# A gated global filter on one core: the exchange read back by halves on alternate partitions, smaller last stores, and a new instruction order

## The chip, the cores and the metric

One core of one Trainium2 chip. The metric is device microseconds of one execution. A run whose time is over 1.5% above the fastest of the same kernel is called slow. The profile covers one execution; its span (first to last instruction) is shorter than that execution's time (before 115.6 against 117.37).

## The reference, cut to what matters

```python
def layer(x, w_r, w_i):                       # _A_ref and _B_ref, alike
    X = rfft2(x.astype(float32))              # x: [1, 2048, 1024] bf16
    return irfft2(X * (w_r + 1j * w_i), s=(2048, 1024)).astype(bfloat16)

def reference(A_x, A_w_r, A_w_i, B_x, B_w_r, B_w_i, gate_w):   # B_x is not used
    g = sigmoid((A_x * gate_w).sum(-1, keepdims=True))
    return g * layer(A_x, A_w_r, A_w_i) + (1 - g) * layer(A_x, B_w_r, B_w_i)
```

## The kernel before

The transforms are matrix products. One string, `ORDER`, lists every operation of the program, some 600 tokens, and each engine runs its share of it in that order. Semaphore waits are put in by the tile framework when the program is built, from what each operation reads and writes. The stages, by token:

- **Folds** `F1, FC, FD, FX, FP`: first transform of x, mirrored columns folded into the tile `y` by VectorE (DVE) and GpSimd (POOL).
- **Unit loop**, 16 units (units 0 to 7 are the even columns, 8 to 15 the odd ones): `F2, T, F3, X` (transform and copies), `P` (product with the weights on DVE), `J` (inverse product on TensorE, PE), `R` (copy of its result to a tile `rl` by ScalarE, ACT, or DVE), `H` (store of `rl` to scratch in DRAM).
- **Exchange**: rows and columns change places between `H` and the read back `L`. Even data goes to the tile `Re`, odd data to `Ro`, in eight blocks of 2,048 columns each.
- **After the loop**: `V` (inverse along rows with the gate masked in, on PE), `VC` (its copy), `C` or `U` (inverse along columns, on PE), `EX, EQ` (even results: a copy, then sum and difference on POOL), `OR, OP, QD, QP` (output rows from even results and odd products), `S` (store of a block).

The parts that the change and the argument touch:

```python
def exchange_row(t, i):
    return 8 * t + 4 * (i % 2) + i // 2
...
    Re = big.tile([P, NS1 * 1024], BF16, name="re")
    Ro = big.tile([P, NS1 * 1024], BF16, name="ro")
    RR = [r[:].rearrange("p (v r s f) -> p v r s f", v=8, r=2, s=2) for r in (Re, Ro)]
    EV = Re[:].bitcast(F32).rearrange("p (v s f) -> p v s f", s=2, v=8)   # even results lie over Re
    SC = [dm.tile([2 * NT, P, 512], BF16, name=f"sc{p}") for p in range(2)]
...
    def scratch_store(n, tt, q="S"):                                      # H
        n, tt = int(n), int(tt)
        a = 4 * (n % NU) + 2 * tt
        Q[q].dma_start(SC[n // NU][a:a + 2].rearrange("a p m -> p a m"), RLs[n][:, tt])

    def scratch_load(par, v, q="S"):                                      # L: 512 KB, all 128 partitions
        par, v = int(par), int(v)
        Q[q].dma_start((Re, Ro)[par][:, v * 2048:v * 2048 + 2048],
                       SC[par][:].rearrange("a (h v q) m -> (a h) v (q m)", h=4, v=8)[:, v])
...
    def even_mix(v, s, h, e):                                             # EQ, on POOL
        t = TM["X", v, s]
        Q[e].tensor_tensor(EV[:, v, s, 256 * h:256 * h + 256], t[:, 0], t[:, 1], (ALU.add, ALU.subtract)[h])
```

When the even data of block v has been used, its even result (f32) is written over the same columns of `Re`. Nearly all DMAs are issued by the sync engine's queue (SP), in the order of the list. A DMA that must wait holds up those behind it: in the changed kernel one read-back waited 3.6 us for POOL and was issued at 81.97 us, and the six stores behind it went out from 82.52 on (80.01 in e1, where that wait is gone).

Of the kernel before, what the change touches and what calls it, by code (L numbers as in the profile page):

```python
# [186 lines left out]
def gated_mix(ctx, tc, x_in, we_in, wo_in, w0_in, gw_in, out):  # L187
# [363 lines left out]
    def scratch_load(par, v, q="S"):  # L551

        par, v = int(par), int(v)
        Q[q].dma_start((Re, Ro)[par][:, v * 2048:v * 2048 + 2048],
                       SC[par][:].rearrange("a (h v q) m -> (a h) v (q m)", h=4, v=8)[:, v])
# [157 lines left out]
```

## Time and profile before

| | before |
|---|---|
| time, median of 3 runs | 117.17 us (117.02 to 118.86) |
| span of the profiled run, granted PE clock | 115.6 us, 0.985 |
| unit loop: last inverse group ends | 77.0 us |
| PE waits for the read-back | 0.8 us, once |
| last DVE row ends; span ends | 112.05; 115.6 us |

The prediction shows the lines. How to read them: in the stretches, one row is a piece of the span with the busy time of each engine, so an engine whose number equals the length of the piece is full. In the waits, a row is "engine, tile, line, what it waited for: us in total, times, longest". In a timeline, the bracket at the end is the idle time of the engine before the group and what ended it.

### The profile page before, as it was taken

The numbers are of one execution on the slowest core, as the hardware profiler recorded it, in microseconds if no ns is written. First come the engines' busy times: TensorE is split into PE (matmuls) and PEld (weight loads), VectorE is DVE, ScalarE is ACT, GpSimd is POOL, SyncE is SP. The second block draws the span as 40 slices with busy tenths as digits, with TensorE's granted clock in tenths as the row PEclk, the third lists the DMA queues.
The fourth block names the chain that finished last, engine by engine and source line by source line (L and its number), as shares of the span: only waits on it lengthen the run. The fifth ranks groups of instructions, "written<-read, shape, count | busy, mean of one in ns | idle before, by whom it ended". The sixth has DMA issues, their size and how long they took to land.

```text
span 115.6 us, 3953 instructions
## 1 busy us (share of the span) xinstructions
...
## 2 busy tenths in 40 slices
...
GB/s 90 348 326 401 403 374 367 363 397 408 210 222 324 371 394 373 169 263 397 350 293 354 348 306 401 254 357 382 352 353 411 403 418 98 198 346 119 327 279 181
DMA packets 17794, 36.79 MB, mean 318 GB/s; under 512 B 1904, under 2 KB 10736, under 8 KB 17776
## 3 DMA queue, kind: packets, MB, share of 16 engines
...
q10 hardware_dynamic: 288, 0.10, 0.4%
...
## 4 chain that ended last, share of the span: by engine, by line
PE 39%; DVE 19%; DMA 16%; ACT 16%; issue 4%; SPq 1%; DVEq 1%; ACTq 0%
ACT rl L204 11%; PE ps L581 9%; PE ps L565 8%; DVE y L382 7%; PE ps L450 6%; PE ps L334 5%; DMA sc<-rl 5%; DMA re<-sc 4%; DMA ig<-cst_ig 4%; PE ps L537 3%; DMA re<-in_x_dram 3%; PE ps L480 3%; DVE p L494 3%; ACT X L204 3%; PE ps L590 3%
## 5 line engine op out<-in xcount | busy, mean ns | idle before, releaser
L615 POOL TENSOR_TENSOR re<-wx 128x256 f32<-128x256 f32 x28 | 19.6, 730 | 55.3 <-DMA re<-sc 53.1
L204 ACT CAST rl<-ps 128x1024 bf16<-128x1024 f32 x29 | 29.6, 1142 | 0.7 <-ACT wx L204 0.7
L204 ACT COPY wx<-ps 128x256 f32<-128x256 f32 (+1 forms) x39 | 17.2, 498 | 10.5 <-PE ps L334 8.2
L537 PE MATMUL ps<-p,wj 32*64 32x512 bf16 x512 | 20.5, 381 | 2.5 <-ACT rl L204 2.0
L204 ACT CAST V<-ps 128x512 bf16<-128x512 f32 x25 | 13.8, 601 | 11.3 <-PE ps L565 8.4
L494 DVE TENSOR_TENSOR p<-X,ro 128x2048 bf16<-128x2048 bf16 x16 | 19.1, 1215 | 0.0
L450 PE MATMUL ps<-fd,y 128*128 128x256 bf16 x128 | 16.5, 273 | 0.4 <-ACT rl L204 0.4
L382 DVE TENSOR_TENSOR y<-ps,wx 128x256 bf16<-128x256 f32 x48 | 16.4, 412 | 0.1
L334 PEld LDWEIGHTS <-re 128*128 128x128 bf16 x256 | 15.2, 100 | 1.6 <-DMA re<-in_x_dram 1.0
L334 PE MATMUL ps<-f,re 128*128 128x128 bf16 x256 | 15.8, 224 | 0.3
L204 ACT CAST T<-ps 128x512 bf16<-128x512 f32 x26 | 15.5, 693 | 0.0
L537 PEld LDWEIGHTS <-wj 32*64 32x64 bf16 x512 | 8.4, 103 | 10.6 <-issue 7.5
L382 POOL TENSOR_TENSOR y<-wx 128x256 bf16<-128x256 f32 x16 | 11.1, 734 | 8.2 <-DVE wx L206 5.9
L635 DVE TENSOR_TENSOR ot<-re,ps 128x512 bf16<-128x512 f32 x22 | 13.8, 681 | 0.4
L450 PEld LDWEIGHTS <-y 128*128 128x128 bf16 x128 | 11.5, 97 | 4.1 <-issue 2.6
L581 PE MATMUL ps<-ig,V 128*128 128x512 bf16 x56 | 13.4, 380 | 0.0
L204 ACT CAST X<-ps 128x1024 bf16<-128x1024 f32 x12 | 13.2, 1118 | 0.0
L206 DVE COPY wx<-ps 128x512 f32<-128x512 f32 (+1 forms) x10 | 5.8, 578 | 7.4 <-PE ps L334 4.8
L480 PE MATMUL ps<-T,wf 64*64 64x256 bf16 (+1 forms) x128 | 10.2, 332 | 1.1 <-DVE np L514 1.0
L590 PE MATMUL ps<-ig,V 128*128 128x256 bf16 x72 | 9.7, 273 | 0.0
L494 DVE TENSOR_TENSOR p<-X,wx 128x2048 bf16<-128x2048 bf16 x8 | 9.4, 1217 | 0.0
L494 DVE TENSOR_TENSOR p<-X,y 128x2048 bf16<-128x2048 bf16 x8 | 9.3, 1215 | 0.0
...
## 6 DMA issues: line engine op xcount, KB each, us to landing
sc<-rl SPq DMA_DIRECT2D x32, 256.0 KB, 4.7
ro<-in_we_dram SPq DMA_DIRECT2D x8, 512.0 KB, 8.3
re<-sc SPq DMA_DIRECT2D x8, 512.0 KB, 6.1
ro<-sc SPq DMA_DIRECT2D x8, 512.0 KB, 7.7
re<-in_x_dram SPq DMA_DIRECT2D x7, 512.0 KB, 8.0
out_dram<-ot SPq DMA_DIRECT2D x7, 512.0 KB, 2.6
wx<-in_wo_dram SPq DMA_DIRECT2D x4, 512.0 KB, 6.6
y<-in_wo_dram SPq DMA_DIRECT2D x4, 512.0 KB, 5.0
```

The source lines that it names most:

```text
L204: nc.scalar.copy(out=out, in_=in_)
L334: nc.tensor.matmul(o, lhsT=lh, rhs=rh, start=(h == 0), stop=(h == 1))
L382: Q[e].tensor_tensor(yo[:, v, k:k + n, s1, :], a.rearrange("p (k c) -> p k c", c=4), b.rearrange("p (k c) -> p k c", c=4), op)
L450: nc.tensor.matmul(ps[:, v * 256:v * 256 + 256], lhsT=y[:, v, par, b, 2 * t:2 * t + 2, :, :].rearrange("p j s c -> p (j s c)"), rhs=C["FD" ...
L480: nc.tensor.matmul(view(ps[ho, tt * 512:(tt + 1) * 512], dst), lhsT=lh, rhs=view(T[hp(jh), tt, :], src), start=(w == 0), stop=(w == 1))
L494: nc.vector.tensor_tensor(p[:, r], xb, w, ALU.mult)
L537: nc.tensor.matmul(o, lhsT=lh, rhs=src[r, ri, wi, tt], start=(q == 0), stop=(q == 3))
L565: nc.tensor.matmul(ps[:, ch * 128:ch * 128 + 128], lhsT=RR[par][:, v, ch // 2, s, c0 + 256 * ab:c0 + 256 * ab + 128], rhs=Ew[:, s1, :], st ...
L581: nc.tensor.matmul(ps, lhsT=Vs[par, v][:, s, ch, :], rhs=rh, start=(ch == 0), stop=(ch == 3))
L590: nc.tensor.matmul(ps[:, o:o + 256], lhsT=Vs[par, v][:, s, ch, :], rhs=g[:, o:o + 256], start=(ch % 2 == 0), stop=(ch % 2 == 1))
L615: Q[e].tensor_tensor(EV[:, v, s, 256 * h:256 * h + 256], t[:, 0], t[:, 1], (ALU.add, ALU.subtract)[h])
L635: nc.vector.tensor_tensor(otile(v)[:, s, h, :], EV[:, v, s], PS["O", 1, v, s], (ALU.add, ALU.subtract)[h])
```

## The change

The intent is to start the read-back earlier. A half of a block needs only the first four of the eight units (or the last four), so it can be issued before the other units are stored. The new row order puts the two halves on alternate partitions; that this moves data faster than two halves of neighbouring partitions was the author's assumption, and e3 tests it. The last block's store is cut in three so that less remains after the last row. The order was made anew around this.

```diff
 def exchange_row(t, i):
-    return 8 * t + 4 * (i % 2) + i // 2
+    r = 8 * t + 4 * (i % 2) + i // 2
+    return 2 * (r % 64) + r // 64
...
-    def scratch_load(par, v, q="S"):
-        par, v = int(par), int(v)
-        Q[q].dma_start((Re, Ro)[par][:, v * 2048:v * 2048 + 2048],
-                       SC[par][:].rearrange("a (h v q) m -> (a h) v (q m)", h=4, v=8)[:, v])
+    def scratch_load(par, v, g, q="S"):
+        par, v, g = int(par), int(v), int(g)
+        Q[q].dma_start((Re, Ro)[par][g:P:2, v * 2048:v * 2048 + 2048],
+                       SC[par][16 * g:16 * g + 16].rearrange("a (h v q) m -> (a h) v (q m)", h=4, v=8)[:, v])
...
-    def store(q, v, s="b"):
+    def store(q, v, s="b", h="b"):        # h: one half of the columns of a row pair
...
 ORDER: the tail of the list (almost every line differs; cut)
-... S:S:3 OR:6:1:0 S:S:6
+... OR:7:0:1 S:S:7:0 OR:7:1:1 S:S:7:1:1 OR:7:1:0 S:S:7:1:0
```

Three small parts: the constant E is loaded in two pieces (120 and 8 partitions), the gate vector's load moves from ACT's queue to SP's, and one pair of mask operations (`GW`) moves from DVE to POOL.

More of the change, by code (lines that the diff above doesn't have):

```diff
@@ L24 @@
 ORDER = """
-warm:8 c:A:F1 c:A:gws tab:A x:S:0:1 x:S:1:1 x:S:2:2 x:S:4:2 x:S:6:2 x:S:8:2 x:S:10:2 x:S:12:2 x:S:14:2 c:S:FD:0:1
-F1:1:o:0 F1:1:e:1 FX:1:o:D F1:0:o:2 FC:1:e:D F1:0:e:3 FP:1:o FD:1:e F1:3:o:0 F1:2:e:4 FC:0:e:D F1:3:e:1 gc:P FD:0:e
-F1:2:o:5 FC:3:e:A FC:2:e:D F1:4:e:3 FD:3:e FX:2:o:A F1:5:o:6 FX:0:o:A FD:2:e F1:5:e:5 FC:4:e:A FP:0:o FX:3:o:A FD:4:e
-F1:6:e:1 FC:5:e:A F1:4:o:2 FD:5:e FC:6:e:A F1:7:e:0 FP:2:o c:S:WF:0:4 FD:6:e F1:6:o:3 W:S:0 FC:7:e:A F1:9:e:7 FD:7:e
-FX:6:o:A F1:8:e:1 FP:3:o FC:9:e:D c:S:WJ:0:4 F1:11:e:3 FD:9:e F1:10:e:0 c:S:w0 FC:11:e:A F1:7:o:4 c:S:PM FC:8:e:A
@@ L30 @@
-FP:6:o FD:11:e FX:5:o:A c:S:EZ F1:13:e:5 FC:10:e:A FD:8:e W:S:1 F1:12:e:6 FP:5:o FD:10:e c:S:WF:4:16 FC:12:e:A
-F1:14:e:1 FC:13:e:A FD:12:e FX:4:o:A F1:15:e:3 W:S:2 F1:15:o:0 FD:13:e FP:4:o FC:15:e:A F1:11:o:2 FC:14:e:A FD:15:e
-FC:15:o:A F1:8:o:6 c:S:WJ:4:16 F1:14:o:5 FD:14:e FC:8:o:A F1:10:o:3 neg:A:0:4 FD:15:o FC:14:o:A F1:12:o:7 FX:7:o:A
-F2:0:0:1 FD:8:o c:S:E FC:10:o:A FP:7:o FC:12:o:A F2:1:0:0 W:S:3 FD:14:o T:0:0:A F2:0:1:4 FC:11:o:A F2:1:1:6 FD:10:o
-T:1:0:A W:S:4 pw:P F1:13:o:1 T:1:1:A FD:12:o F1:9:o:0 T:0:1:A F3:1:5 FD:11:o c:S:FD:1:2 FC:9:o:A F3:0:3 FC:13:o:A
@@ L35 @@
-FD:9:o X:1:A W:S:5 F2:3:1:2 FD:13:o F2:2:0:7 X:0:A F2:3:0:0 P:1:0 W:S:6 Y:1:1 F2:2:1:5 T:3:0:A Y:0:3 neg:A:4:16 GH:4
-P:1:1 W:S:7 T:2:0:A T:2:1:A NA:1:D N:1:D P:0:0 T:3:1:A GC:A NA:0:D P:0:1 F3:2:0 F2:4:0:5 X:2:A F2:4:1:2 F3:3:6 J:1:3:0
-T:4:0:D T:4:1:A X:3:A P:2:0 Y:2:2 GT:0:5 R:1:0:A F2:5:0:6 Y:3:7 NA:2:D P:2:1 T:5:0:A H:1:0 F3:4:2 c:S:IG R:1:1:A
-GT:1:5 W:S:8 F2:5:1:4 N:0:D NA:3:D P:3:0 X:4:A J:0:6:0 W:S:9 T:5:1:A H:1:1 N:2:D GT:2:5 P:3:1 R:0:0:A Y:4:2 GT:3:5
-F3:5:3 W:S:10 R:0:1:A N:3:D H:0:0 F2:7:1:6 GK:D NA:4:D P:4:0 F2:6:1:2 X:5:A GZ:0:0 F2:6:0:5 P:4:1 GS:0 W:S:11 F2:7:0:7
@@ L40 @@
-T:7:0:A T:7:1:D J:2:3:0 T:6:0:A GW:D:4 T:6:1:A Y:5:6 GW:D:0 R:2:0:A N:4:D NA:5:D P:5:0 R:2:1:A H:2:0 W:S:12 H:0:1
-P:5:1 F3:7:6 J:3:2:4 X:7:A H:2:1 F3:6:0 R:3:0:A F2:8:0:6 X:6:D F2:8:1:7 R:3:1:A F2:9:0:2 Y:7:3 T:8:0:D Y:6:0 T:8:1:A
-GZ:1:4 NA:6:D T:9:0:A P:7:0 J:4:6:0 GS:1 F2:9:1:2 N:5:D P:7:1 R:4:0:A T:9:1:A H:4:0 P:6:0 J:5:4:6 W:S:13 R:4:1:A H:3:0
-NA:7:D N:7:D R:5:0:A H:4:1 P:6:1 F3:8:2 F3:9:0 R:5:1:A F2:11:1:4 X:8:D F2:10:0:5 X:9:A H:5:1 F2:10:1:6 H:3:1 N:6:D
-F2:11:0:7 W:S:14 P:8:0 T:10:0:A J:6:2:0 T:11:0:A T:11:1:A T:10:1:D R:6:0:A P:8:1 J:7:4:6 R:6:1:A H:6:0 F3:10:2 H:5:0
@@ L45 @@
-P:9:0 R:7:0:A P:9:1 R:7:1:A H:7:0 J:8:0:4 X:10:A GW:D:12 H:7:1 F2:12:0:6 H:6:1 F2:12:1:7 W:S:15 R:8:0:A T:12:0:D
-P:10:0 R:8:1:A J:9:2:0 P:10:1 T:12:1:A H:8:1 F3:11:4 H:8:0 R:9:0:A F2:13:1:6 X:11:D R:9:1:A H:9:0 F3:12:2 F2:14:0:7
-X:12:A H:9:1 F2:13:0:0 L:0:0 F2:14:1:1 L:0:1 T:13:0:A T:13:1:D P:11:0 L:0:2 J:10:4:2 L:0:3 T:14:0:A P:11:1 T:14:1:A
-F3:13:6 R:10:0:A P:12:0 X:13:A H:10:0 J:11:0:4 L:0:4 P:12:1 R:10:1:A F3:14:6 R:11:0:A X:14:D F2:15:0:2 F2:15:1:3
-T:15:0:A P:13:0 T:15:1:A J:12:0:6 R:11:1:A V:0:0:1:2 P:13:1 R:12:0:A F3:15:4 V:0:0:0:3 R:12:1:D X:15:A H:12:0
@@ L50 @@
-V:0:1:0:0 H:10:1 V:0:1:1:1 L:0:5 VC:0:1:0:A P:14:0 H:11:0 J:13:4:6 VC:0:0:0:A VC:0:1:1:A P:14:1 VC:0:0:1:A R:13:0:A
-P:15:0 J:14:0:2 R:13:1:A H:13:0 H:11:1 C:0:0:1:4 P:15:1 H:12:1 C:0:0:0:5 EX:0:0:D R:14:0:D R:14:1:A EX:0:1:A H:14:1
-J:15:6:2 H:13:1 EQ:0:1:0:P V:0:2:0:4 EQ:0:0:0:P C:0:1:1:5 R:15:0:D R:15:1:A H:14:0 C:0:1:0:0 EQ:0:0:1:P H:15:1
-V:0:2:1:1 VC:0:2:0:A GW:D:8 V:0:3:1:2 H:15:0 EX:1:1:A L:0:6 V:0:3:0:3 VC:0:2:1:A EX:1:0:D L:0:7 EQ:1:1:0:P C:0:2:0:4
-VC:0:3:0:D VC:0:3:1:A C:0:2:1:1 EQ:1:0:0:P V:0:4:1:0 EX:2:1:D EQ:0:1:1:P V:0:4:0:5 C:0:3:0:2 EQ:2:1:0:P VC:0:4:0:A
@@ L55 @@
-C:0:3:1:1 EX:2:0:A V:0:5:0:3 EQ:1:1:1:P VC:0:4:1:A V:0:5:1:5 EQ:1:0:1:P VC:0:5:0:A C:0:4:0:4 VC:0:5:1:A EQ:2:0:0:P
-L:1:0 C:0:5:0:0 EX:4:0:D L:1:1 C:0:4:1:3 L:1:2 E:3:0:D EQ:4:0:0:P L:1:3 V:0:6:0:5 EX:4:1:A L:1:4 C:0:5:1:4 L:1:5
-EQ:2:0:1:P VC:0:6:0:D V:0:6:1:2 L:1:6 EX:5:0:D EQ:4:0:1:P V:0:7:1:3 VC:0:6:1:A V:0:7:0:5 EX:5:1:A EQ:5:0:0:P C:0:6:0:0
-L:1:7 C:0:6:1:2 EQ:2:1:1:P EX:6:1:A EQ:5:1:0:P VC:0:7:0:A VC:0:7:1:D E:3:1:D C:0:7:1:3 V:1:0:0:1 V:1:0:1:4 EQ:4:1:0:P
-VC:1:0:0:A C:0:7:0:2 VC:1:0:1:D EX:6:0:A EQ:6:1:0:P U:1:0:0:1 EX:7:0:A EQ:6:1:1:P V:1:1:0:0 OC:0:0:A EQ:5:0:1:P
@@ L60 @@
-V:1:1:1:2 VC:1:1:0:D U:1:0:1:4 EQ:6:0:0:P V:1:2:0:5 EQ:7:0:0:P V:1:2:1:0 VC:1:2:0:A EQ:7:0:1:P U:1:1:0:1 VC:1:2:1:D
-VC:1:1:1:A EQ:4:1:1:P EX:7:1:A U:1:2:0:5 OP:0:0:0 OR:0:1:1 OC:1:0:A OR:0:1:0 U:1:1:1:0 OR:2:0:0 EQ:6:0:1:P V:1:3:0:1
-U:1:2:1:4 OP:0:0:1 VC:1:3:0:A V:1:3:1:2 V:1:4:0:1 OP:1:0:0 OR:1:1:0 OR:2:0:1 OR:2:1:1 S:S:0 VC:1:3:1:A OR:1:1:1
-C:1:3:0:3 VC:1:4:0:A V:1:4:1:5 OR:2:1:0 EQ:7:1:0:P C:1:3:1:0 VC:1:4:1:A QD:3:0:0 S:S:2 U:1:4:0:1 OP:1:0:1 QD:3:1:1
-V:1:5:0:2 QD:3:1:0 OC:4:0:A V:1:5:1:4 EQ:5:1:1:P S:S:1 VC:1:5:0:A QD:3:0:1 U:1:4:1:5 OP:4:0:0 VC:1:5:1:D U:1:5:0:0
@@ L65 @@
-OR:4:1:0 OP:4:0:1 U:1:5:1:1 OR:5:0:0 OR:4:1:1 V:1:7:0:4 QP:3:0:0:P V:1:6:1:2 OR:5:0:1 S:S:4 VC:1:7:0:A V:1:7:1:3
-OR:5:1:1 U:1:7:0:4 VC:1:7:1:A EQ:7:1:1:P OR:5:1:0 V:1:6:0:0 QP:3:1:1:P OR:7:0:0 S:S:5 U:1:7:1:1 VC:1:6:0:A OR:7:0:1
-VC:1:6:1:A QP:3:1:0:P U:1:6:0:0 S:S:7:0 OR:7:1:1 OR:7:1:0 U:1:6:1:2 QP:3:0:1:P OR:6:0:0 S:S:7:1 OR:6:1:1 OR:6:0:1
-S:S:3 OR:6:1:0 S:S:6
+warm:8 c:A:F1 tab:A x:S:0:1 x:S:1:1 x:S:2:2 x:S:4:2 x:S:6:2 x:S:8:2 x:S:10:2 x:S:12:2 x:S:14:2
+c:S:FD:0:1 F1:0:e:0 F1:0:o:1 FC:0:e:A F1:1:e:2 FX:0:o:D FC:1:e:D F1:3:e:3 FD:0:e F1:3:o:1 FD:1:e F1:1:o:4
@@ new lines @@
+FX:3:o:A F1:2:e:0 FX:1:o:D FP:3:o F1:2:o:2 FC:2:e:A F1:5:e:1 FD:2:e F1:4:e:4 FC:5:e:A FP:0:o F1:4:o:5
+FC:3:e:A FD:5:e FC:4:e:A F1:7:e:0 FD:4:e F1:6:e:6 FP:1:o c:S:WF:0:4 FD:3:e FC:6:e:A F1:9:e:1 W:S:0
+FC:7:e:A F1:8:e:4 FD:6:e FC:9:e:A F1:6:o:3 FC:8:e:A FD:9:e c:S:WJ:0:4 F1:10:e:7 FX:4:o:A F1:7:o:6 FD:7:e
+c:S:w0 FP:4:o FC:10:e:A F1:11:e:1 c:S:PM FX:6:o:A FD:10:e F1:5:o:0 c:S:gws FX:2:o:A FD:8:e F1:13:e:3
+c:S:EZ FC:11:e:A FP:2:o F1:12:e:2 FD:11:e FC:13:e:A F1:15:e:7 FD:13:e F1:14:e:4 FP:6:o FC:15:e:A F1:14:o:1
@@ new lines @@
+FD:15:e FC:14:e:A F1:11:o:3 W:S:1 FX:5:o:A FD:14:e F1:9:o:5 c:S:WF:4:16 FC:12:e:A FP:5:o FC:14:o:A F1:13:o:0
+FC:11:o:A FD:12:e FX:7:o:A F1:10:o:4 W:S:2 FD:11:o FC:9:o:A F1:12:o:7 FP:7:o FC:13:o:A c:S:WJ:4:16 F2:1:0:2
+FC:10:o:A FD:14:o FC:12:o:A F1:8:o:3 c:S:E T:1:0:A FD:10:o F2:0:0:6 gc:P W:S:3 neg:A:0:4 F2:0:1:1
+FC:8:o:A FD:9:o T:0:0:A F2:1:1:2 W:S:4 FD:12:o T:0:1:A F1:15:o:4 pw:P T:1:1:A FD:8:o F3:0:5
+FC:15:o:A F3:1:1 FD:13:o c:S:FD:1:2 X:0:A F2:2:0:3 FD:15:o W:S:5 F2:2:1:7 X:1:A F2:3:0:0 P:0:0
@@ new lines @@
+Y:0:6 T:2:0:A GH:4 W:S:6 T:3:0:A NA:0:D P:0:1 neg:A:4:16 W:S:7 T:2:1:A F2:3:1:5 N:0:D
+P:1:0 GC:A F3:2:0 T:3:1:A J:0:2:6 c:S:IG X:2:A P:1:1 F3:3:4 R:0:0:A GT:0:0 P:2:0
+GT:3:0 Y:1:1 R:0:1:A Y:2:2 F2:5:0:3 P:2:1 X:3:A F2:4:0:6 F2:5:1:7 NA:1:D NA:2:D T:5:0:A
+N:2:D P:3:0 J:2:4:1 T:4:0:A T:5:1:A GT:1:0 N:1:D R:2:0:D R:2:1:A H:2:1 P:3:1 F3:5:6
+F2:7:0:3 X:5:A GT:2:0 J:1:1:4 W:S:8 GK:A H:0:0 F2:4:1:0 T:7:0:D R:1:0:A Y:3:6 Y:5:7
+T:4:1:D F2:7:1:3 R:1:1:A NA:3:D NA:5:D F3:4:0 N:3:D P:5:0 F2:6:0:2 T:7:1:A H:1:1 J:3:4:6
@@ new lines @@
+H:0:1 T:6:0:A P:5:1 W:S:9 X:4:A GZ:0:2 N:5:D R:3:0:A R:3:1:D F3:7:0 X:7:A H:3:0
+F2:6:1:4 P:4:0 H:1:0 Y:4:5 GZ:1:6 GS:0 W:S:10 NA:4:D H:2:0 P:7:0 T:6:1:A W:S:11
+J:5:0:2 GS:1 H:3:1 P:4:1 F3:6:4 R:5:0:A F2:9:1:6 W:S:12 N:4:D F2:9:0:7 GW:D:4 F2:8:0:0
+T:9:0:D T:9:1:A R:5:1:A W:S:13 Y:7:1 NA:7:D P:7:1 F3:9:6 X:6:A F2:8:1:1 N:7:D X:9:A
+GW:D:0 J:7:2:4 T:8:0:D T:8:1:A F2:11:1:6 P:6:0 R:7:0:A F2:11:0:7 H:7:0 P:6:1 J:4:0:2 H:5:0
+H:5:1 T:11:0:D T:11:1:A R:7:1:A Y:6:6 R:4:0:A NA:6:D N:6:D P:9:0 R:4:1:A P:9:1 F3:11:4
@@ new lines @@
+J:6:0:6 X:11:A H:4:1 F2:13:1:2 L:0:0:0 F2:13:0:3 R:6:0:A L:0:1:0 F3:8:4 P:11:0 H:4:0 X:8:A
+L:0:2:0 F2:10:0:0 P:11:1 H:7:1 F2:10:1:1 R:6:1:A T:13:0:D T:13:1:A H:6:1 J:11:4:6 T:10:0:A T:10:1:D
+H:6:0 P:8:0 L:0:3:0 J:9:2:0 R:11:0:A W:S:14 R:11:1:D R:9:0:A P:8:1 F3:10:4 X:10:A H:9:0
+F2:12:1:6 H:11:0 F2:12:0:7 R:9:1:A F3:13:2 P:10:0 T:12:0:A H:9:1 J:8:4:0 GW:D:12 T:12:1:A W:S:15
+X:13:A L:0:0:1 P:10:1 F2:15:0:7 H:11:1 F2:15:1:6 R:8:0:A L:0:1:1 F3:12:2 R:8:1:D L:0:4:0 T:15:0:A
+F2:14:0:4 T:15:1:A L:0:2:1 P:13:0 F2:14:1:5 X:12:A J:10:0:6 L:0:3:1 P:13:1 T:14:0:A L:0:4:1 F3:15:2
@@ new lines @@
+R:10:0:A P:12:0 T:14:1:A L:0:5:1 X:15:A V:0:0:0:4 L:0:5:0 P:12:1 F3:14:0 R:10:1:A V:0:0:1:5 VC:0:0:0:D
+VC:0:0:1:A H:10:1 J:13:2:6 P:15:0 X:14:A H:8:0 H:8:1 C:0:0:0:4 P:15:1 R:13:0:A L:0:6:1 C:0:0:1:5
+H:10:0 EX:0:0:A J:12:0:2 P:14:0 H:13:0 EX:0:1:A EQ:0:1:0:P V:0:2:0:4 R:13:1:D R:12:0:A V:0:1:0:5 EQ:0:0:0:P
+VC:0:1:0:A V:0:1:1:0 VC:0:2:0:D H:13:1 EQ:0:1:1:P R:12:1:A V:0:2:1:1 L:0:6:0 P:14:1 J:15:4:6 EQ:0:0:1:P VC:0:2:1:A
+H:12:1 VC:0:1:1:A H:12:0 R:15:0:A R:15:1:D J:14:2:0 GW:P:8 H:15:0 C:0:1:0:4 R:14:0:D R:14:1:A H:15:1
@@ new lines @@
+C:0:2:1:5 C:0:1:1:6 EX:1:0:A H:14:1 C:0:2:0:7 EX:1:1:D EX:2:1:A H:14:0 V:0:3:0:0 EQ:1:0:0:P EX:2:0:A L:0:7:0
+V:0:4:0:1 EQ:1:1:0:P VC:0:3:0:A L:0:7:1 V:0:3:1:6 V:0:4:1:7 L:1:0:0 EQ:2:0:0:P VC:0:3:1:A C:0:3:0:0 L:1:1:0 EQ:2:1:0:P
+C:0:3:1:6 E:3:0:A V:0:5:1:2 EQ:2:1:1:P VC:0:4:0:A VC:0:4:1:D V:0:5:0:0 EQ:1:1:1:P C:0:4:0:1 VC:0:5:0:A VC:0:5:1:D C:0:4:1:3
+EQ:1:0:1:P EX:4:0:D C:0:5:1:2 L:1:0:1 EX:4:1:A V:0:6:1:0 EQ:4:0:0:P L:1:1:1 EX:5:1:A C:0:5:0:1 L:1:2:0 EQ:4:1:0:P
+V:0:6:0:3 L:1:3:0 V:0:7:0:2 L:1:2:1 EQ:4:0:1:P VC:0:6:0:A VC:0:6:1:D E:3:1:D V:0:7:1:0 L:1:3:1 VC:0:7:0:A C:0:6:1:4
@@ new lines @@
+EQ:4:1:1:P L:1:4:1 VC:0:7:1:D C:0:6:0:3 L:1:4:0 EQ:5:1:0:P EX:5:0:D C:0:7:0:2 C:0:7:1:0 EQ:2:0:1:P EX:6:1:D EX:7:0:A
+V:1:0:0:1 L:1:5:0 EX:6:0:A EQ:5:0:0:P V:1:0:1:5 VC:1:0:0:D L:1:5:1 V:1:1:0:2 EQ:5:0:1:P VC:1:0:1:A V:1:1:1:3 VC:1:1:0:D
+U:1:0:0:1 EQ:5:1:1:P VC:1:1:1:A EQ:6:1:0:P U:1:0:1:2 OC:0:0:A EQ:6:0:0:P U:1:1:1:3 EQ:6:0:1:P U:1:1:0:1 EQ:6:1:1:P V:1:2:0:4
+OP:0:0:0 OR:0:1:0 OR:0:1:1 EX:7:1:D OC:1:0:A V:1:3:1:2 VC:1:2:0:A V:1:3:0:0 OP:0:0:1 V:1:2:1:1 VC:1:3:0:A U:1:2:0:4
+VC:1:3:1:A OP:1:0:0 OR:1:1:1 OR:1:1:0 VC:1:2:1:D S:S:0 C:1:3:0:0 OR:2:0:0 L:1:6:1 C:1:3:1:1 L:1:6:0 QD:3:0:0
@@ new lines @@
+U:1:2:1:5 OP:1:0:1 L:1:7:0 QD:3:1:0 V:1:4:0:2 QD:3:1:1 V:1:5:0:3 QP:3:0:0:P S:S:1 VC:1:4:0:A V:1:4:1:6 QD:3:0:1
+L:1:7:1 U:1:4:0:1 OR:2:0:1 VC:1:4:1:A QP:3:0:1:P VC:1:5:0:A OR:2:1:1 U:1:4:1:0 OR:2:1:0 V:1:5:1:4 QP:3:1:1:P S:S:2
+U:1:5:0:5 VC:1:5:1:A OC:4:0:A V:1:6:0:2 QP:3:1:0:P U:1:5:1:3 VC:1:6:0:A V:1:6:1:1 OP:4:0:0 OR:4:1:1 OR:4:1:0 OR:5:0:0
+OR:5:0:1 S:S:3 OR:5:1:0 U:1:6:0:0 VC:1:6:1:A OR:5:1:1 EQ:7:0:0:P V:1:7:0:2 S:S:5 OR:6:0:0 U:1:6:1:1 OP:4:0:1
+VC:1:7:0:A OR:6:0:1 V:1:7:1:3 OR:6:1:0 U:1:7:0:0 EQ:7:0:1:P S:S:4 VC:1:7:1:A OR:6:1:1 EQ:7:1:0:P U:1:7:1:2 S:S:6
@@ L69 @@
+OR:7:0:0 EQ:7:1:1:P OR:7:0:1 S:S:7:0 OR:7:1:1 S:S:7:1:1 OR:7:1:0 S:S:7:1:0
 """
@@ L259, in load_c @@
             Q[q].dma_start(C[n][:], gw_in)
+        elif n == "E":
+            for g in (slice(0, 120), slice(120, P)):
+                Q[q].dma_start(C[n][g], dr[n][g])
         elif n == "w0":
```

6 lines of the change are left out of this document (5 added, 1 removed).

## The prediction

> **What bounds the kernel now.** The cores view shows one core, 115.6 us, clock 0.985, so no throttle matters. I read the busy time by stretch first. The cuts are the first VectorE (DVE) work (5.94), the end of the folds (23), the start of the last group of inverse products (L537, near 77), the landing of the last even read-back (85) and the last stretch of TensorE (PE) work.
>
> ```profile
> 23.00:77.00 54.00, 49.94 (x988) 29.44 (x981) 53.02 (x73) 53.40 (x73) 0.86 (x3) 1.00 0.94 325
> 77.00:85.00 8.00, 7.79 (x103) 6.87 (x100) 5.38 (x9) 5.68 (x11) 6.89 (x11) 1.00 1.06 366
> 85.00:108.30 23.30, 22.68 (x237) 16.32 (x238) 17.72 (x29) 11.99 (x23) 22.24 (x27) 1.00 0.72 288
> 108.30:115.60 7.30, 1.73 (x8) 0.58 (x6) 3.67 (x6) 0.26 (x1) 2.09 (x2) 0.76 0.66 262
> ```
>
> The columns are PE, weight loads, DVE, ScalarE (ACT), GpSimd (POOL), then clock, DMA share, GB/s. There are three stages with three limits. From 23 to 77, the loop over the 16 units, DVE (53.0 of 54) and ACT (53.4) are both full; PE's 49.9 is waiting between short groups. From 77 on PE is full (30.5 of 31.3) while DVE and ACT have gaps, and POOL, idle in the loop, is full after 85. From 108 on nothing but the tail runs. So the end is: loop (ACT and DVE), then PE work left over, then tail. Next, the waits by cause and the queue's own waits:
>
> ```profile
> POOL re L615 <- DMA re<-sc: 53.1, 1, 53.1
> PEld L565 <- DMA re<-sc: 1.1, 1, 1.1
> PE ps L565 <- DMA re<-sc: 0.8, 1, 0.8
> SPq L554 <- DMA sc<-rl: 1.9, 1, 1.9
> ```
>
> The exchange through memory (tile sc) costs PE 0.8 us once; a second wait, 1.9 us, sits in the queue before the odd read-back, hidden behind even work. POOL's 53.1 us is no loss. Then the tail, in order of time:
>
> ```profile
> 103.12 8.93 DVE L635 TENSOR_TENSOR ot<-re,ps 128x512 bf16<-128x512 f32 x14
> ...
> 106.64 3.75 POOL L647 TENSOR_TENSOR ot<-pq 128x512 bf16<-128x512 f32 x3
> ...
> 107.24 2.79 PE L581 MATMUL ps<-ig,V 128*128 128x512 bf16 x12
> ```
>
> PE ends at 107.24 + 2.79 = 110.03, POOL at 110.39, DVE at 103.12 + 8.93 = 112.05; the span ends 3.55 us later. So three engines end within 2 us, and shortening one alone is not worth its full amount. The last store's share of the tail is in the DMA rows:
>
> ```profile
> out_dram<-ot SPq DMA_DIRECT2D x7, 512.0 KB, 2.6
> out_dram<-ot SPq DMA_DIRECT2D x2, 256.0 KB, 2.0
> ```
>
> [...] The stores above differ by 0.6 us for 256 KB[...]; their fixed part is 2.0 - 0.6 = 1.4 us[...], and I use that.
>
> **The change part by part.** The arithmetic is the same (3,240 rows on PE in both); what changes is the build order and the transfers.
>
> *Read back by halves.* 16 loads of 512 KB become 32 of 256 KB, with 4 KB rows as before, so the bytes are the same. The low half needs only units 0 to 3 (or 8 to 11): in the built order four even low halves now stand ahead of the last even store. The added cost is 16 issues of some 0.4 us on the sync queue, which spent 25.9 us waiting for ACT's rl copies, so it is hidden. The gain: the 0.8 us wait of PE should go, and the odd data should be there in time. One thing works against it: in the built program the halves of the last two even blocks wait for POOL's writes to the same tile, at other columns (4 to 8 POOL results must be there first; before, none). POOL starts near 72 to 76, the sixth result and the moved mask work take 6 x 0.7 + 2.5 = 6.7 us, a load 4 us, so they land near 83 to 87, close to when PE wants them. I take 0.6 us of the 0.8.
>
> *Loop order.* I counted the instructions up to the last inverse group in both orders, and took spacings from back-to-back runs in the timeline: on ACT rl 0.89 us, X 0.90, T 0.47, large and small fold copies about 0.5 and 0.3; on DVE rl 1.13, X 1.14, T 0.6, V 0.61, folds' copies 0.6 and 0.38. ACT: 4 rl fewer (-3.5), 4 X more (+3.6), 1 T fewer (-0.5), 3 small fold copies more and 1 large fewer (+0.4), 1 other copy and the gate column more (+0.7): +0.7. DVE: 4 rl more (+4.5), 4 X fewer (-4.6), 1 T more (+0.6), fold copies -0.5, 2 V more, 1 even copy and the gate column fewer (+0.5): +0.5. Both are full, so the loop ends some 0.5 us later by sums. They have 1.0 and 0.6 us of gaps, and the new order spreads the store and copy chain better (the fourth inverse group comes after 4 us less ACT work), so I give back 0.3: net +0.2.
>
> *PE work after the loop.* Groups after the last inverse group: 28 V groups before, 26 after (16 matmuls in 0.89 us make two groups, 0.445 each); the 16 split and 14 full cosine-sine groups stay. That is -0.9 us on PE, which is the limit there.
>
> *Start.* PE now begins with row block 0, the first to be loaded, instead of block 1; it waited 1.0 us for block 1 until 4.87. But DVE's first copy now comes after the second group, not the first. DVE's copies in the folds are 0.5 us fewer, already counted. I take -0.2.
>
> *POOL.* One pair of masks (two 128x512 operations) moves from DVE to POOL: 2 x 1.28 by its rows of that size, 2.5 us. Its output work begins some 4 us earlier in the order (after the first even group, with ACT at 76.0 instead of 81.3 us of listed work), but four results in and it must wait for PE's next even groups. Its 24 remaining results, 6 sums and 4 pair rows make 17.5 + 7.7 + 5.2 = 30.4 us; from about 78.5 that ends at 109, a little earlier than now, and its last result now feeds the last rows of DVE. So POOL limits the gain.
>
> *Last stores.* The last one goes from 512 KB (2.6 us) to 128 KB: 1.4 + 0.3 = 1.7, so -0.9 us. DVE still does two rows after PE's last group. The split of E into 120 and 8 partitions, and gws to another queue, are off the path.
>
> Sum: -0.6 + 0.2 - 0.9 - 0.2 - 0.9 = -2.4 us if all add; I take off 0.3 because POOL and DVE end close to PE. That makes 117.17 - 2.1 = 115.1.
>
> **Rivals.** *The DVE tail takes over.* From its first output row at 94.94 DVE is full to 112.05. Its row work after the change is one copy of 0.7 us longer, and the first row comes 0.9 us of PE work earlier, so it cancels: if PE gains more than that, DVE still ends at 111.5 and only the store's 0.9 us and part of the start remain, giving 115.9. *Early read-back crowds the stores.* The DMA share is 0.94 in the loop and above 1 around 80; loads pushed between stores delay them (4.7 us to landing now), the five rl buffers come free later, and ACT waits. There were such steps (3.0 us at 50.3 on the chain of waits) with little ACT idle. If it costs 1.5 us, 116.6. *More than the sums.* If the better order also lets PE do more of its work inside the loop (49.9 us busy there for far less at its pipelined pace), PE could end 2 us earlier still and the time would be 113.5. Against it: ACT and DVE have no room for the copies. *POOL or the false wait stalls PE.* 1 to 2 us lost, so 116 to 117.
>
> **Range and chances.** Two per cent below 117.17 is 114.83, only 0.3 us under my figure, so the verdict is nearly open. The rivals that lose give 115.9 to 117, the one that gains 113.5: range 113.5 to 116.7. Faster by over 2%: 0.43; within 2%: 0.53; slower by over 2%, which needs a new stall of 4 us: 0.04.
>
> **What would show it.** Right: the PE wait on re<-sc gone or under 0.3 us; the last inverse group at 77 within 1 us; PE's last group ending near 108.7; last DVE row to span end about 2.6 instead of 3.55 us. Wrong: a wait of PE or of the queue for POOL over 1 us, ACT idle in the loop on sc<-rl, gaps of DVE over 1.5 us between its output rows, or a loop that ends over 1 us earlier, which my sums exclude.

## The result

The changed kernel takes 131.99 us (median of 4 runs, 130.63 to 133.47, one of them slow); before took 117.09 in the same set of runs. The ratio is 1.125 (95% interval 1.113 to 1.136): slower, by far more than the range allowed. All ratios here are the mean time of one kernel's fast runs over that of the kernel before in the same rounds, so not quite the ratio of the medians. Results are correct.

The cores view of the changed kernel gives a span of 130.0 us at clock 0.943. Next its stretches, with cuts at its own stages; columns as in the prediction (PE, weight loads, DVE, ACT, POOL, clock, DMA share, GB/s):

```profile
23.00:66.00 43.00, 38.80 (x768) 23.15 (x767) 42.40 (x64) 42.00 (x58) 1.43 (x7) 1.00 0.90 314
66.00:69.90 3.90, 1.84 (x47) 0.68 (x44) 3.90 (x4) 3.90 (x7) 0.00 (x0) 1.00 1.07 403
69.90:74.00 4.10, 3.04 (x36) 2.05 (x44) 2.54 (x4) 0.94 (x3) 0.00 (x0) 0.60 1.04 416
74.00:84.50 10.50, 9.97 (x192) 6.44 (x191) 8.36 (x8) 10.11 (x15) 2.87 (x3) 0.99 0.66 218
84.50:97.30 12.80, 4.35 (x41) 3.91 (x41) 1.38 (x2) 1.87 (x5) 5.27 (x7) 0.76 0.68 216
97.30:125.60 28.30, 28.07 (x261) 20.02 (x263) 20.91 (x34) 13.31 (x24) 26.55 (x31) 0.93 0.65 236
```

Until 66 us the loop is what it was: DVE and ACT full. Then come two holes. From 69.9 to 74, PE, DVE and ACT all fall back, and the clock is 0.60. From 84.5 to 97.3, 12.8 us, no engine is half busy: PE 4.35, DVE 1.38, ACT 1.87, POOL 5.27, and the DMA share is 0.68. After 97.3 PE is full as before, though until 101.5 at a granted clock of 0.50. When every engine idles together, each waits for another, so the waits come next:

```profile
POOL re L626 <- DMA re<-sc: 6.9, 2, 3.6
ACT re L212 <- DMA re<-sc: 5.9, 1, 5.9
PE ps L576 <- ACT re L212: 4.8, 1, 4.8
PE ps L576 <- DMA re<-sc: 3.1, 1, 3.1
PE ps L576 <- DMA sc<-rl: 2.7, 1, 2.7
PE ps L576 <- POOL eb L451: 1.0, 1, 1.0
```

And the queue's own waits:

```profile
SPq L565 <- POOL re L626: 9.3, 3, 3.6
```

L626 is an even result being written (`EQ`), L212 a copy on ACT (here the even result of block 3), L565 a read-back, L576 a `V` product. Read the two fences together: even results wait for read-backs, and read-backs wait for even results. Before, no read-back waited for POOL, and the only long wait of the even results was the first one, for their work to begin. In order of time, POOL:

```profile
79.07 2.87 POOL L626 TENSOR_TENSOR re<-wx 128x256 f32<-128x256 f32 x3 [54.64 <-DMA sc<-rl]
85.23 0.72 POOL L626 TENSOR_TENSOR re<-wx 128x256 f32<-128x256 f32 x1 [3.29 <-DMA re<-sc]
85.91 1.15 POOL L450 TENSOR_TENSOR ea<-ea,e 128x512 bf16<-128x512 bf16 x1
87.14 1.15 POOL L451 TENSOR_TENSOR eb<-e,ea 128x512 bf16<-128x512 bf16 x1
88.25 0.72 POOL L626 TENSOR_TENSOR re<-wx 128x256 f32<-128x256 f32 x1
92.05 0.72 POOL L626 TENSOR_TENSOR re<-wx 128x256 f32<-128x256 f32 x1 [3.08 <-DVE V L214]
96.41 3.45 POOL L626 TENSOR_TENSOR re<-wx 128x256 f32<-128x256 f32 x5 [3.64 <-DMA re<-sc]
```

And the sync queue over the same time:

```profile
74.05 4.21 SPq L560 DMA_DIRECT2D sc<-rl  x3
81.97 0.46 SPq L565 DMA_DIRECT2D re<-sc  x1
82.52 4.04 SPq L560 DMA_DIRECT2D sc<-rl  x6
89.00 4.26 SPq L565 DMA_DIRECT2D re<-sc  x2
93.31 5.06 SPq L565 DMA_DIRECT2D ro<-sc  x8
```

Now the hole can be followed. Three results of block 0 are done at 79.07 + 2.87 = 81.94. At 81.97 the queue, which stood still until then with stores behind it, issues the read-back of block 6, which waited 3.6 us for POOL. The fourth result of block 0 waits 3.29 us for that read-back to land (85.23). Two masks that PE needs stand behind it on POOL. The six stores that were held up go out from 82.52 on (80.01 in e1, where that wait is gone). At 88.97 the next result is done, and at 89.00 the queue issues the next read-back, and so on three times. (For the result at 92.05 the trace names a copy of `V`. In the built program that result waits for a copy that was done at 84.27 and for the read-back issued at 89.00, so it was the read-back.) The chain of what ended last, before the end of the hole:

```profile
91.06 0.70 DVE V L214
...
92.05 0.73 POOL re L626
...
92.80 3.48 DMA re<-sc
...
96.66 0.59 ACT re L212
...
97.29 1.01 PE ps L576 x8
```

A result on POOL, a read-back, a copy on ACT that writes another block's result, and then PE. The odd read-back begins at 93.31; before it began at 83.95. The tail behaved as the prediction said: the last DVE row ends at 116.53 + 10.77 = 127.30, 2.7 us before the end (predicted 2.6), and the last stores landed in 1.7 us, as predicted:

```profile
out_dram<-ot SPq DMA_DIRECT2D x2, 128.0 KB, 1.7
116.53 10.77 DVE L646 TENSOR_TENSOR ot<-re,ps 128x512 bf16<-128x512 f32 x17
```

In the built programs I counted semaphore waits between a read-back into `Re` and a write of an even result to **other** columns of `Re`: none before, 21 after (18 of a result for a read-back, 3 of a read-back for a result). I call them crossing waits. No byte is shared in any of them. What has changed for the waits' maker is the shape of the read-back: every second partition instead of all.

### The profile page after: what moved, and what is told of

Read it like the earlier page. It is cut to its first block, busy times and chain, and to the rows that moved or that the text cites. A ratio compares the mean times of both kernels' runs of the same rounds, so it can differ in the third digit from the quotient of the medians.

```text
span 130.0 us, 3989 instructions
## 1 busy us (share of the span) xinstructions
PE 107.1 (82%) x1616; PEld 74.2 (57%) x1619; DVE 97.5 (75%) x161; ACT 85.5 (66%) x139; POOL 49.2 (38%) x76
## 5 line engine op out<-in xcount | busy, mean ns | idle before, releaser
L626 POOL TENSOR_TENSOR re<-wx 128x256 f32<-128x256 f32 x28 | 20.3, 756 | 65.5 <-DMA sc<-rl 54.6
L212 ACT CAST rl<-ps 128x1024 bf16<-128x1024 f32 x25 | 25.6, 1048 | 0.8 <-PE ps L548 0.8
L212 ACT COPY wx<-ps 128x256 f32<-128x256 f32 (+1 forms) x41 | 17.3, 487 | 13.2 <-PE ps L345 7.8
L212 ACT CAST V<-ps 128x512 bf16<-128x512 f32 x23 | 13.1, 590 | 17.4 <-PE ps L576 15.7
L548 PE MATMUL ps<-p,wj 32*64 32x512 bf16 x512 | 19.0, 382 | 1.9 <-ACT rl L212 0.5
L576 PE MATMUL ps<-ea,re 128*128 128x128 bf16 x64 | 10.9, 257 | 10.6 <-ACT re L212 4.8
L576 PEld LDWEIGHTS <-re 128*128 128x128 bf16 x128 | 10.1, 117 | 13.3 <-issue 12.6
L212 ACT CAST X<-ps 128x1024 bf16<-128x1024 f32 x16 | 16.6, 1045 | 0.3 <-PE ps L491 0.2
L345 PEld LDWEIGHTS <-re 128*128 128x128 bf16 x256 | 15.3, 101 | 1.7 <-DMA re<-in_x_dram 1.2
L214 DVE CAST V<-ps 128x512 bf16<-128x512 f32 x9 | 6.2, 692 | 12.8 <-PE ps L576 11.9
L212 ACT CAST T<-ps 128x512 bf16<-128x512 f32 x25 | 14.7, 642 | 0.1
L214 DVE COPY wx<-ps 128x512 f32<-128x512 f32 (+1 forms) x8 | 5.1, 652 | 11.8 <-PE ps L601 6.3
L491 PE MATMUL ps<-T,wf 64*64 64x512 bf16 (+1 forms) x128 | 10.8, 345 | 1.5 <-DVE T L214 1.4
```

The costliest lines, as they stand in the source:

```text
L212: nc.scalar.copy(out=out, in_=in_)
L214: Q[e].tensor_copy(out=out, in_=in_)
L345: nc.tensor.matmul(o, lhsT=lh, rhs=rh, start=(h == 0), stop=(h == 1))
L491: nc.tensor.matmul(view(ps[ho, tt * 512:(tt + 1) * 512], dst), lhsT=lh, rhs=view(T[hp(jh), tt, :], src), start=(w == 0), stop=(w == 1))
L548: nc.tensor.matmul(o, lhsT=lh, rhs=src[r, ri, wi, tt], start=(q == 0), stop=(q == 3))
L576: nc.tensor.matmul(ps[:, ch * 128:ch * 128 + 128], lhsT=RR[par][:, v, ch // 2, s, c0 + 256 * ab:c0 + 256 * ab + 128], rhs=Ew[:, s1, :], st ...
```

## The experiments

The theory (A in the texts): the crossing waits are most of the loss, and they come from the partition step of the half loads. Its rivals: the half loads or their rows as such are slow, or the new order is. After the first four runs a second question stood, the 2.5 us beyond the crossing waits: is it that the early low halves crowd the queue (D), or what the halves cost themselves?

| run | median us | before us | ratio (95% interval) |
|---|---|---|---|
| e1 after, even results in `y` | 119.83 | 117.44 | 1.022 (1.011 to 1.032) |
| e2 after, whole loads | 117.06 | 117.44 | 0.997 (0.990 to 1.003) |
| e3 after, contiguous halves | 124.19 | 117.44 | 1.055 (1.046 to 1.065) |
| e4 before, alternate halves | 124.40 | 117.44 | 1.059 (1.052 to 1.066) |
| e5 e1, even halves joined | 119.48 | 117.62 | 1.016 (1.010 to 1.022) |
| e6 e5, one low half early | 118.34 | 117.62 | 1.008 (1.002 to 1.013) |
| e7 e4, even results in `y` | 118.55 | 117.62 | 1.011 (1.005 to 1.017) |
| e8 e6, first `V` group later | 119.30 | 117.62 | 1.014 (1.008 to 1.020) |
| e9 e2, even results in `y` | 117.66 | 117.35 | 1.008 (1.002 to 1.015) |
| e10 before, last store in three | 118.46 | 117.35 | 1.015 (1.008 to 1.022) |
| e11 e10, one block read earlier | 118.70 | 117.35 | 1.017 (1.010 to 1.024) |
| e12 after, loads before results | 122.27 | 117.35 | 1.036 (1.023 to 1.050) |

All twelve gave correct results. In the last set (e9 to e12) four slower runs of before, of 11, are counted as slow, which puts the mean of its fast runs at 116.8 and the ratios of e9 to e11 some 0.5% above what the medians say. Two of e12's four runs are slow, so its ratio rests on two runs.

**e1: the even results in another tile.** The tile `y` is free by then. Nothing else changes; no crossing wait is left in the built program.

```diff
-    EV = Re[:].bitcast(F32).rearrange("p (v s f) -> p v s f", s=2, v=8)
+    y32 = y[:].bitcast(F32).rearrange("p v e b t s c -> p v e (b t s c)")
+    EVs = [y32[:, (i % 4) // 2, 1 - i // 4, (i % 2) * 1024:(i % 2) * 1024 + 1024].rearrange("p (s f) -> p s f", s=2) for i in range(8)]
...    EV[:, v, s ...]  ->  EVs[v][:, s ...]  everywhere
```

> The changed kernel with the even results kept in tile y, which is free by then, instead of in re: the half read-backs then share no tile with the results. Theory A (in the built program the strided half loads of re and the writes of the even results to other columns of re wait for each other; that is the stretch from 84.5 to 97.3 us in which TensorE works 4.35 us): the stretch closes, 119 to 123 us. Theory B (small transfers on alternate partitions are slow in themselves): still 128 or more. Theory C (the new order is bad as such): 127 or more.

Measured: 119.83 us. The second hole is gone, and with it 12 us: the ratio falls from 1.125 to 1.022. The first hole stays:

```profile
70.00:74.00 4.00, 2.95 (x36) 1.80 (x44) 3.09 (x4) 1.51 (x3) 0.00 (x0) 0.69 1.03 408
71.05 0.22 PE L577 MATMUL ps<-ea,re 128*128 128x128 bf16 x1 [2.83 <-DMA re<-sc]
73.59 1.69 PE L549 MATMUL ps<-p,wj 32*64 32x512 bf16 x32
```

PE waits 2.8 us for the first high half, and then 32 inverse products take 1.69 us at a lower clock. The wait is for data, and the clock follows: 1.00 from 66 to 70, 0.69 from 70 to 74, 0.89 from 74 to 78.

**e2: whole loads.** The changed order with the old row order and the old 512 KB loads, each at the place of its later half.

```diff
-    r = 8 * t + 4 * (i % 2) + i // 2
-    return 2 * (r % 64) + r // 64
+    return 8 * t + 4 * (i % 2) + i // 2
...  scratch_load as before;  L:par:v:0 ... L:par:v:1  ->  L:par:v at the later of the two places
```

> The changed kernel with the old row order and whole 512 KB read-backs, each at the place of its later half; order and all else stay. A: no crossing waits are left in the program, 118 to 123 us, close to e1. B: the transfers are as before, 117 or less. C: the order alone costs it, 127 or more.

Measured: 117.06 us, the same as before. So the new order, the last stores, the masks and the new queues together are worth nothing that can be measured, and the whole loss of 15 us belongs to the halves with their row order (the new row order with whole loads was not tried). Its lines for the same moment as in e1, and its last DVE group:

```profile
70.00:74.00 4.00, 3.81 (x88) 2.19 (x84) 4.00 (x5) 3.69 (x6) 0.00 (x0) 1.00 1.03 412
69.24 0.23 PE L561 MATMUL ps<-ea,re 128*128 128x128 bf16 x1 [1.53 <-DMA re<-sc]
70.90 1.07 PE L533 MATMUL ps<-p,wj 32*64 32x512 bf16 x32
101.73 10.85 DVE L631 TENSOR_TENSOR ot<-re,ps 128x512 bf16<-128x512 f32 x17
```

PE waits 1.5 us instead of 2.8, the clock stays at 1.00, and the same 32 products take 1.07 us. DVE's last row ends at 112.58 (before 112.05), and the span ends 2.7 us later: the smaller last store's gain is spent on a tail that ends later.

**e3: contiguous halves.** Halves stay, on partitions 0 to 63 and 64 to 127, with the old row order.

```diff
-        Q[q].dma_start((Re, Ro)[par][g:P:2, v * 2048:v * 2048 + 2048],
+        Q[q].dma_start((Re, Ro)[par][64 * g:64 * g + 64, v * 2048:v * 2048 + 2048],
...  exchange_row as before
```

> The changed kernel with the old row order and the halves loaded into partitions 0 to 63 and 64 to 127. The built program has no crossing waits[...]. A: 119 to 123 us as e1, plus up to 3 us[...] (landing well over the 5.4 us of the changed kernel). B: no better than the changed kernel, 128 or more. C: 127 or more.

Measured: 124.19 us. Its built program has no crossing wait either, so the partition step is what makes them. But it pays in another way:

```profile
70.00:74.00 4.00, 0.01 (x1) 0.04 (x2) 0.96 (x1) 1.27 (x2) 0.00 (x0) 0.95 1.05 246
74.00:78.00 4.00, 4.00 (x61) 2.37 (x62) 2.89 (x3) 0.99 (x2) 0.00 (x0) 0.63 1.04 215
```

The DMA share is full (1.05, 1.04) at 246 and 215 GB/s, where e1 and e2 move 408 and 412 from 70 to 74 at the same share (1.03). An even half takes 7.5 us to land (median of 16), against 5.4 in e1 and in the changed kernel. The first wait of PE grows to 5.7 us.

**e4: halves in the order before.** Each load of before is replaced by its two alternate halves at the same place; nothing else.

```diff
 ...  L:0:0  ->  L:0:0:0 L:0:0:1  (all 16);  exchange_row and scratch_load of the change
```

> The kernel before with only the read-back changed: both halves on alternate partitions, issued at the old places; old order otherwise. The built program has 18 crossing waits. A: 120 to 127 us, with the results of even rows waiting for loads of re. B: some slower, 118 to 121, with loads taking longer to land. C: as before, 116.5 to 118.

Measured: 124.40 us, 7 us slower than before, with 18 crossing waits in the built program. The order before had no trouble until the loads were cut, and then had the same trouble:

```profile
POOL re L610 <- DMA re<-sc: 7.1, 1, 7.1
DVE re L201 <- DMA ro<-sc: 3.0, 1, 3.0
```

The second row is DVE writing an even result to `Re`. The trace names an odd read-back, but in the built program this write waits for even halves of blocks 3 and 5 to 7, and it starts at 88.61 us, when POOL's 7.1 us wait ends too (88.55). The names of DMA releasers are inferred.

**e7: e4 with the even results in `y`.** The same edit as e1, on e4.

> e4 with the even results in y: the kernel before with both halves on alternate partitions at the old places and no crossing waits. A with D: 116.5 to 118, like the kernel before. E: 119 or more. If moving the results to y brought anything by itself, below 116.5.

Measured: 118.55 us, 1.011. Of e4's 5.9%, 4.8 are the crossing waits. So the theory holds in both orders.

**e5: even halves joined.** e1, with each even low half moved down next to its high half.

```diff
 ...  L:0:v:0 (early)  ->  directly ahead of L:0:v:1, for every even block v
```

> e1 (even results in y) with each early even low half moved to stand beside its high half, so both halves go out where e2 has its whole load; odd halves as in the changed kernel. Theory D (what e1 still loses against e2 is that 1 MB of early low halves stands in a full queue before the last weights and the first high half, so the first second-stage group of TensorE waits 2.8 us instead of 1.5 and the clock then drops): 116 to 117.5 us, that wait at 1.5 us or less, clock 1.00 from 70 to 74. Theory E (256 KB transfers on alternate partitions cost more than 512 KB ones): 119 to 120 as e1.

Measured: 119.48 us. The crowding theory had expected 116 to 117.5, so this is a miss in the time. In the trace the clock did stay at 1.00 between 70 and 74, as that theory said, but PE now waits twice for the read-back:

```profile
PE ps L564 <- DMA re<-sc: 3.5, 2, 1.9
```

The first wait, for block 0, is 1.59 us (e1: 2.83; e2: 1.53), close to what the theory said. The second, 1.94 us at 89.88, is for block 7; e1 had none there, and e2 0.51. So the gain at block 0 was given back at block 7, and this is what the theory had not seen.

**e6: only block 0's low half early.** The other even halves stay joined.

> e5 with the low half of block 0 alone left at its early place (256 KB ahead instead of 1 MB). D: the first high half needs only 256 KB to land, so 115.5 to 117.5 and a wait under 1.5 us. E: 119 to 120.

Measured: 118.34 us. PE's waits for the read-back fall from 2.8 us (e1) and 3.5 us (e5) to 1.1 us (0.15 for block 0, 0.91 for block 7):

```profile
PE ps L564 <- DMA re<-sc: 1.1, 2, 0.9
```

At block 0 the order is clear, in one profiled execution each: one early half, 0.15 us; none, 1.59; the four of the change, 2.83. In time it is less so: the ratio is 1.008 against e1's 1.022, some 1.6 us of 117, but these are two sets of runs whose intervals overlap a little, and e5 without any early half (1.016) is hardly faster than e1.

**e8: the first `V` group later.** e6, with the first two `V` products and their copies moved behind an inverse group.

```diff
-... V:0:0:0:4 ... V:0:0:1:5 VC:0:0:0:D VC:0:0:1:A H:10:1 J:13:2:6 P:15:0 X:14:A
+... H:10:1 J:13:2:6 P:15:0 X:14:A V:0:0:0:4 V:0:0:1:5 VC:0:0:0:D VC:0:0:1:A
```

> e6 with the first two second-stage groups of TensorE placed after the next inverse group, so that the loop is not held up behind their read-back. D: the wait on the read-back is gone and ACT and DVE stay full to about 77; 114.5 to 117. If ACT and DVE are the limit anyway: as e6.

Measured: 119.30 us, not better than e6, so a miss for D. The wait for block 0 is gone, as expected; PE's one wait for a read-back is now 1.76 us at 89.18, for block 7 (0.91 in e6). The loop still ended at 79.4 us (79.0 in e6), not near 77. As in e5, taking a wait away at block 0 did not shorten the whole.

**e9: what the move to `y` costs.** e2 with the edit of e1, as a control, since there is no crossing wait to remove.

> e2 (whole loads, new order) with the even results in y, a control for the moved results. If the move is free: 116.5 to 117.8, as e2, and what e1, e5, e6 and e7 lose against it is the half loads. If keeping the results in y costs time itself: 118.5 to 120, as e1 and e5.

Measured: 117.66 us, 1.008, against 0.997 for e2. The move may itself cost up to 1%; part of this is the lower base of that set of runs. In the profiled run (the slowest of six) PE waited 1.41 us for block 7 against 0.51 in e2; why is open. Two things follow. The crossing waits cost at least the 12 us of e1. And e7's 1.1% cannot be put down to the halves: with the even results in `y`, whole loads (e9) show about as much.

**e10 and e11: the last store alone.** Before, with the store of its last block in 256, 128 and 128 KB (e10), and with the even read-back of block 6 moved up as well (e11).

```diff
-... OR:6:0:1 S:S:3 OR:6:1:0 S:S:6
+... OR:6:0:1 S:S:6:0 S:S:3 S:S:6:1:1 OR:6:1:0 S:S:6:1:0
(e11)  L:0:6 moved to just behind L:0:5
```

> The kernel before with only its last store (block 6, 512 KB) cut to one of 256 KB and two of 128 KB. By the landing times, 2.6 us against 1.7, the tail should shrink by 0.9 us: ratio 0.990 to 0.996. If the tail is set elsewhere: ratio 1.00.

> e10 with the even read-back of block 6 issued right after that of block 5, ahead of the last odd stores. It should take away the 0.8 us wait of TensorE at 85.6: ratio to before 0.980 to 0.990. If the queue is full, the later stores and the odd read-back come later by as much: as e10.

Measured: 118.46 and 118.70 us, both slower than before, both misses. In e10 the row of the last stores reads:

```profile
out_dram<-ot SPq DMA_DIRECT2D x2, 128.0 KB, 2.7
```

So a 128 KB store takes 2.7 us to land here, against 1.7 in the changed kernel. In this order stores of 512 and 256 KB are issued just ahead of the two small ones, which is the likely reason. That takes the gain of the smaller size. The rest of the loss is mostly in the tail too: the last row ends at 112.42 us (before 112.05), but the two small stores are issued only from 112.70 on, in 1.46 us (0.93 in the changed kernel), and the span ends 4.5 us after the last row instead of 3.55. In e11 it is 4.5 us as well. So the cut stores stood behind others in the queue; a run that changes only their place was not made.

**e12: read-backs before results.** The changed kernel, with the last three even half loads moved ahead of the first even result. Results may still wait for read-backs (17 crossing waits), but no read-back can wait for a result.

```diff
-... L:0:6:1 ... L:0:6:0 ... L:0:7:0 ... L:0:7:1
+... L:0:6:1 L:0:6:0 L:0:7:0 L:0:7:1
```

> The changed kernel with its last three even half loads placed ahead of the first even result; results stay in re. The loads then wait for no result, but the results still wait for all loads to land. Theory A with the exchange of waits in both directions as the large part: one wait of some 5 us in place of three exchanges, 121 to 125. If the waits of the queue for GpSimd hardly matter: 129 or more.

Measured: 122.27 us (fast runs 121.80 and 120.12), 1.036, as expected. In the stretch of the hole, 84.5 to 97.3, PE is busy 11.21 us instead of 4.35; POOL starts at 81.49 us (77.40 in e1), one delay instead of three. Of the loss of 12.5%, 8.8 points go when the waits run one way only, and 1.5 more in e1, when they are gone (this last step is within the intervals). The cost is the exchange, result to read-back to result, each round a landing of 3 to 3.6 us (POOL's waits of 3.29, 3.08 and 3.64 above) and the whole queue behind it; waits in one direction cost far less, 3.6% against 12.5%.

## Why the prediction was wrong

In ratios to before: the change 1.125; crossing waits one way only 1.036 (e12); none 1.022 (e1); early low halves joined but one 1.008 (e6); whole loads 0.997 (e2). That is about 12 us for the crossing waits, some 1.6 us for the crowding (the least certain of the steps), and the last 1.1% between the move to `y`, the halves themselves and noise, which these runs don't part.

- **The step that failed** is "POOL or the false wait stalls PE. 1 to 2 us lost". The mechanism was seen, in one direction: "the halves of the last two even blocks wait for POOL's writes to the same tile". It was sized as one delay, 6.7 us of POOL work and a 4 us landing. The other direction, the results of block 0 waiting for read-backs, was not looked for. With both, it is a ping-pong, three landings in a row with the in-order queue and POOL's masks behind it: 12 us by e1. The sign that the prediction had named, a wait of the queue for POOL over 1 us, came at 9.3 us. The doubt was stated ("a new stall of 4 us") and given a chance of 0.04.
- **"POOL starts near 72 to 76"**: it started at 79.07. In the built program its first result waits for seven half loads of other blocks, the last of them issued at 73.41. (The trace names a store as the releaser; such names are inferred.) Without crossing waits (e1) it still started at 77.40, so most of this delay is the late loop.
- **"I take 0.6 us of the 0.8"** for PE's wait on the read-back: it grew to 3.1 us. The four early low halves (1 MB) were issued between 54 and 60 us, ahead of the last two loads of weights, and the high half that completes block 0 came behind all of them. In e1 it was issued at 64.46 and let PE go on at 71.05, 6.6 us later; in e6, with one early half, at 63.67 and 68.08, 4.4 us later. "Early read-back crowds the stores" was among the rivals; what it crowded was the read-back itself. The wait is shown (2.83 us against 0.15); the 1.6 us of time is the difference of e1 and e6. The DMA engines were not idle then (on e1's page the DMA share is in the tenths 8 and 7 from 53.1 to 59.0 us, at 280 and 236 GB/s, and 9 from 59.0 to 62.0, at 357), and the four early halves brought nothing.
- **Loop order, net +0.2**: until 66 us the loops agree (DVE 42.40 against 42.15 busy). The last inverse group then ended at 82.1 instead of 77.0 (the prediction: 77 within 1 us). With whole loads (e2) it ended at 79.2, so the step was short by 2 us even without the halves. PE's wait of 1.5 us in that stretch is not most of it: in e6, where it is 0.15 us, that group ended at 79.0. The rest stays open.
- **Start, -0.2**: DVE's first copy began at 6.30 us, later than the 5.94 before. Wrong in sign, and small.
- **Last stores, -0.9, and 1.7 us to land**: right in the changed kernel (tail 2.7 instead of 3.55, landing 1.7). Its fixed part of 1.4 us was an estimate from the two landings before, 2.6 us for 512 KB and 2.0 for 256 KB. In e10, with larger stores just ahead, it took 2.7 us and the tail 4.5.
- **"The DVE tail takes over"**: e2 confirms this rival. With the halves undone, DVE ends at 112.58 and the time is 117.06; it had been put at 115.9 (from its own parts, 111.5 for DVE and 0.9 for the store, it would be 115.7).
- **The row order on alternate partitions** was right in its purpose: e3 without it is 4.4 us slower than e1 and moves 246 GB/s where e1 moves 408 (70 to 74 us). It is this partition step, though, that makes the waits.
- **Masks on POOL**, 2 x 1.28: they took 1.15 each. Right in size, but they stood behind a waiting result, and PE waited 1.0 us for them.

The clock adds to it. In the changed kernel it is 1.00 from 66 to 70 us, 0.50 from 71 to 74, after PE's wait of 3.1 us, and 1.00 again from 75 to 84. Over stretches of about 4 us it is 0.60 there, 0.69 in e1 after 2.8 us and 0.64 in e12 after 3.6, but 1.00 in e2 after 1.5 us and in e5 after 1.9. So the clock fell after these waits for a read-back of 2.8 us and more and not after those of 1.9 and less; where between them it begins to fall, these runs don't show. After the 4.8 us wait that ends the large hole the clock is 0.50 from 97.3 to 101.5, with PE busy all 4.2 us. The 128x128 `V` products of the changed kernel start 0.107 us apart at clock 0.50 (71.02 to 71.66) and 0.056 at 1.00 (77.44 to 78.28), so at 1.00 that work would take about half as long, and up to 2.1 us of the 12 are clock, by my estimate from these figures.

## What to carry to other kernels

When a transfer is cut by partitions with a step, look at what else lives in that tile, in both directions, and count the waits in the built program. A buffer that is reused column by column is only free column by column if the waits' maker sees it so; here two tiles (e1, 1.022) cost less than a wait that runs both ways through an in-order queue (1.125). And look at what an earlier transfer pushes back in the same queue: here four early halves delayed the one half that was needed first (6.6 us from its issue until PE went on in e1, 4.4 in e6 with one early half).

## What these runs show of waits, clock and transfers

- DMAs with a partition step were made to wait for accesses to other columns of the same tile, and these for them: 21 such waits in the changed kernel, 12 us (e1); none with contiguous halves (e3) or whole loads (e2).
- A gap of 2.8 us was followed by a clock of 0.69 over the stretch of 4 us, and 32 products took 1.69 instead of 1.07 us (e1, e2); after a gap of 1.5 us the clock was 1.00 (e2).
- Contiguous halves moved 215 to 246 GB/s, where alternate halves and whole loads moved 408 to 412 (e3; e1, e2). Alternate halves did not always keep this rate: from 86 to 95 us, while it read back the odd halves, e7 moved 322 GB/s (share 0.93), where before moved 407 with whole loads (1.02). Whether the size or the step does it stays open.
- Halves brought no gain: e1 (1.022) is slower than whole loads, e2 (0.997), and e7 (1.011) no faster than before. The larger cost was in the waits, 12 us.
- Stores from the sync queue: 512 KB landed in 2.6 us and 256 KB in 2.0 (before), 128 KB in 1.7 in the changed kernel. As an estimate from these, 0.6 us for each 256 KB and a fixed part near 1.4. With stores ahead of them, 128 KB took 2.7 us (e10).
